# Sliding-window attention into a mixture of attention experts: outputs as rows of tokens with the key sum as a 65th column, fp32 turns, 128-key score products and 768-byte rows of q and k

## The chip, the cores and the metric

The program runs on one core of one Trainium2 chip. The metric is the device time of one execution in microseconds, as the median over runs. A core has TensorE (PE, with its weight loads shown apart as PEld), VectorE (DVE), ScalarE (ACT), GpSimd (POOL) and SyncE (SP), which here issues the DMAs.

## The reference

Eight batches of 576 tokens; the first layer has eight heads of 64, the second four experts with heads of 64.

```python
# layer 1: sliding window, per batch and head
scores = q @ k.T / 8                      # where |i - j| <= 32, else -1e9
attn = softmax(scores);  y = attn @ v
x = y of all heads side by side           # (8, 576, 512)
# layer 2: gate and experts
logits = x @ w_gate                       # 4 experts, the best 2 per token, softmax over the 2
for e in range(4):
    a = softmax(causal((x @ wq[e]) @ (x @ wk[e]).T / 8))
    out += weight_of_e * (a @ (x @ wv[e])) @ wo[e]
```

Everything is float32 outside. The first layer and the gate are computed in fp32, the experts in bf16 with fp32 sums.

## The kernel before

The kernel is written as named steps, and the string `ORDER` lists them in the order in which they are emitted. Every engine works through its own instructions in that order, so `ORDER` also fixes what TensorE does next and which DMA SP issues next. A step such as `S.4.1:21` is "scores of group 4, half 1"; the digits behind the colon choose which of four PSUM slots of two banks each it uses. `wN` is N warm-up products. The function `step` beside each name holds a planner's costs and dependencies; they were used to find the order and don't run on the chip. Groups are i = 2b + g: batch b, four heads each.

The steps of the first layer, with b the batch:

- `load.i.qn` and `load.i.kn` (L138, four DMAs each, on SP): one group's q or k goes to SBUF as `nat`, 32 partitions a head, in rows of two tokens (512 bytes). Groups 0 and 1 come in two parts.
- `turn` (L285): DVE turns 32 x 32 blocks, four instructions a load, so that head dimensions lie on partitions.
- `S.i.half` (L305): per half of 288 queries, products of 64 keys with 64 to 160 queries, each in two pieces of 32 head dimensions; heads take the four row groups of the array, even and odd 64-key blocks its two column halves. Then exp on ACT (L311) and the band mask, a multiply on POOL (L313; on DVE for groups 0 and 1).
- `loadv` (L152, L154, five DMAs) and `dup` (L162 on ACT, L164 on POOL): V in tiles of 128 keys, and copies shifted by 64 so that every span of queries finds its 128 keys on 128 partitions.
- `SUM.b` (L321): the sums over keys, 32 products with one-hot weights, then a reciprocal on DVE. For batches 0 to 3 the reciprocals are split into three bf16 parts (L330 to L335).
- `U.i.x` (L364): output of two heads as 64 dimensions by queries, eight segments of 64 or 96 queries each, V as weights.
- For batches 0 to 3 `U` is copied by ACT (L373), and `N.i.x` spreads the reciprocals over partitions with a selecting product (L384) and multiplies on DVE (L386). For batches 4 to 7 (`SPREAD`) the reciprocals go to DRAM and come back broadcast over 64 partitions (`Ro`, `Ri`; RD and RB), and DVE multiplies straight from PSUM (L368).
- Both leave XTF, the layer's output in fp32 with dimensions on partitions, which the gate reads, and a bf16 copy XTB by POOL (L378) for the experts.

The second layer's steps are `G1` and `G3` (the gate), `QK` and `V` (projections, L450, L472), `PS` (scores and exp, L492, L495), `AV` (L518), `PT` (turns in bf16, L540) and `Y` (output projection, L551, copy by ACT, L556, and the DMA out). `WL` and `WC` load and cast the experts' weights (L245 to L264), once. fp32 products are written as one call and appear in the trace as two matmul records.

Of the kernel before, what the change touches and what calls it, by code (L numbers as in the profile page):

```python
# [8 lines left out]
F32 = mybir.dt.float32  # L9
BF16 = mybir.dt.bfloat16  # L10
# [24 lines left out]
    dup.2.0.3 S.6.0:02 dup.2.0.0 load.7.kn.0 PS.1.0.1:1 AV.0.1:3 SUM.2:2 dup.3.0.3 dup.2.0.2 PS.1.1.0:1
    PS.1.0.2:3 load.8.kn.0 turn.7.kn.0 U.5.1:0 U.4.0:1 PT.0.0:3 dup.3.0.0 load.7.qn.0 S.6.1:02 load.8.qn.0
    U.4.1:1 turn.7.qn.0 N.4.0:0 PS.1.1.1:2 N.5.1:3 U.5.0:1 PS.1.0.3:2 turn.8.kn.0 load.9.kn.0 S.7.0:30
    N.4.1:2 U.6.0:1 PS.1.1.2:0 PT.0.1:3 turn.8.qn.0 N.5.0:2 AV.1.0:1 S.7.1:03 loadv.4.0 G1.2:2 QK.2.0.0:0
    load.10.kn.0 G3.2 S.8.0:31 QK.2.0.1:0 turn.9.kn.0 U.6.1:3 PS.2.0.0:0 load.9.qn.0 turn.9.qn.0 PS.1.1.3:1
    SUM.3:2 S.8.1:10 load.11.kn.0 V.2.0:3 WL.o PS.2.0.1:0 S.9.0:21 PS.2.0.2:0 AV.1.1:3 load.10.qn.0 U.7.0:1  # L40
    V.2.1:0 WC.o QK.2.1.0:2 turn.10.qn.0 PT.1.0:0 turn.10.kn.0 S.9.1:31 QK.2.1.1:2 PS.2.0.3:3 U.7.1:0
    N.6.1:2 PS.2.1.0:3 N.7.0:1 PT.1.1:0 N.7.1:2 load.12.qn.0 N.6.0:3 load.12.kn.0 PS.2.1.1:1 SUM.4:0
    dup.4.0.0 load.11.qn.0 PS.2.1.2:3 QK.3.0.0:1 loadv.5.0 Ro.4 G1.3:2 dup.4.0.2 dup.4.0.3 V.3.0:1
    PS.2.1.3:3 dup.4.0.1 G3.3 QK.3.0.1:0 QK.3.1.0:3 S.10.0:21 turn.11.qn.0 PS.3.0.0:3 load.13.kn.0
    QK.3.1.1:0 V.3.1:2 dup.5.0.2 AV.2.0:1 Ri.4 PS.3.0.1:2 Y.0.0:0 U.8.1:3 PS.3.1.0:1 PS.3.0.2:0 U.8.0:2
    turn.11.kn.0 S.10.1:13 Y.0.2:2 U.9.0:0 S.11.0:31 PS.3.0.3:0 U.9.1:2 PS.3.1.1:3 turn.12.kn.0 load.13.qn.0
# [16 lines left out]
"""  # L63


MASKS = ["DVE"] * 2 + ["POOL"] * 14
DUP = ["ACT", "POOL", "ACT", "POOL"]

SPREAD = (4, 5, 6, 7)

S = 576
HS = 288


@with_exitstack
def kernel(
# [12 lines left out]
    nc = tc.nc  # L89
# [31 lines left out]


    nat = {}
    vsb = {}


    def parts(i):
        return [(0, 5), (5, 9)] if i < 2 else [(0, 9)]
# [577 lines left out]
```

## Time and profile before

| what | before |
|---|---|
| median of 6 runs | 285.15 us (282.73 to 286.09) |
| the profiled execution's own time | 286.83 us |
| its span | 285.1 us |
| PE busy, share of the span | 261.1 us, 92% |
| DVE, ACT, POOL busy | 167.6, 154.3, 145.6 us |
| mean granted TensorE clock | 0.968 |
| moved by DMA | 45.48 MB in 91,800 packets |

The span runs from the first to the last instruction of the program. A busy PE is not a PE at its peak: matmuls are pipelined and their ends are modelled. In the chain of waits "SPq" is time in which the chain hangs on SP's queue of DMA issues, "issue" time in which the engine waited for nothing that the profile shows. Where a stretch is given as A:B, both are microseconds from the start of the span.

### The profile page before, as it was taken

What the parts mean: (1) busy time and instruction counts of PE and PEld (TensorE: products, weight loads), DVE (VectorE), ACT (ScalarE), POOL (GpSimd) and SP (SyncE); (2) the same over time, 40 slices, a digit from 0 to 9 for tenths busy, and PEclk for the clock granted to TensorE, in tenths of its full rate; (3) what the DMA queues carried; (4) which work ended last, traced back from release to release, by engine and by line L of the source; (5) the groups of instructions that cost most, each with busy time, mean ns of one, the idle gap of its engine ahead of it and who ended that gap; (6) DMA issues with size and microseconds to landing.
All of it is one profiled execution on the core that took longest, in us unless ns stands there. A gap on an engine that the chain in (4) does not pass through costs nothing.

```text
span 285.1 us, 12971 instructions
## 1 busy us (share of the span) xinstructions
PE 261.1 (92%) x5723; PEld 188.6 (66%) x5723; DVE 167.6 (59%) x448; ACT 154.3 (54%) x226; POOL 145.6 (51%) x202
## 2 busy tenths in 40 slices
PE   8967959996999799979999999999999999999873
PEld 2533837775787677867776787687768677856520
DVE  5735772364884767757576576448784167454610
ACT  1443333883467773446757643936574753377242
POOL 7103065916759667584644965767545932322200
PEclk9997997998999999999999999999999999999959
DMA  4647999999999758999873596899471204411126
GB/s 127 157 126 190 204 157 214 208 200 202 198 206 191 118 111 180 196 207 147 166 203 126 167 232 115 254 258 226 94 222 41 78 22 143 175 74 57 57 117 215
DMA packets 91800, 45.48 MB, mean 160 GB/s; under 512 B 47840, under 2 KB 84832, under 8 KB 91744
## 3 DMA queue, kind: packets, MB, share of 16 engines
q1 hardware_dynamic: 91744, 44.66, 69.5%
q8 instruction: 44, 0.72, 1.2%
q14 instruction: 12, 0.10, 0.1%
HBM read 35.14 MB, written 9.51 MB: 157 GB/s over the span
## 4 chain that ended last, share of the span: by engine, by line
PE 67%; SPq 17%; DMA 5%; issue 4%; DVE 4%; ACT 2%; ACTq 0%; DVEq 0%
PE u L364 11%; PE sc L305 10%; SPq L138 9%; PE pp L450 9%; PE po L518 8%; PE py L551 7%; PE ps L492 6%; PE pv L472 5%; PE sums L321 4%; DMA kn<-in_k_dram 3%; SPq L152 3%; PE pg L406 3%; PE pt L540 2%; SPq L245 2%; DMA qn<-in_q_dram 2%
## 5 line engine op out<-in xcount | busy, mean ns | idle before, releaser
L313 POOL TENSOR_TENSOR AT<-AT,MASKP 128x576 f32<-128x576 f32 x56 | 77.6, 1408 | 32.9 <-ACT AT L311 32.8
L495 ACT ACTIVATE ATE<-ps 128x1024 bf16<-128x1024 f32 (+1 forms) x64 | 53.0, 837 | 30.9 <-PE ps L492 28.0
L311 ACT ACTIVATE AT<-sc 128x576 f32<-128x576 f32 x64 | 38.1, 648 | 43.6 <-PE sc L305 41.3
L305 PE MATMUL sc<-Tqn,Tkn 32*64 32x128 f32 (+3 forms) x2560 | 48.1, 271 | 9.2 <-DVE Tkn L285 3.9
L305 PEld LDWEIGHTS sc<-Tqn,Tkn 32*64 32x64 f32 x2560 | 41.1, 132 | 17.8 <-issue 7.7
L364 PE MATMUL u<-AT,vsb 128*64 128x64 f32 (+1 forms) x1024 | 40.2, 234 | 5.2 <-issue 5.1
L364 PEld LDWEIGHTS u<-AT,vsb 128*64 128x64 f32 x1024 | 35.1, 140 | 10.1 <-issue 8.2
L378 POOL CAST XTB<-XTF 128x576 bf16<-128x576 f32 x32 | 21.1, 665 | 28.3 <-DVE XTF L368 15.1
L285 DVE STREAM_TRANSPOSE Tkn<-kn 128x288 f32<-128x288 f32 (+2 forms) x72 | 25.5, 412 | 8.4 <-DMA kn<-in_k_dram 8.4
L499 POOL TENSOR_SCALAR_AFFINE_SELECT ATE<-ATE 128x384 bf16<-128x384 bf16 x32 | 15.9, 521 | 26.8 <-ACT ATE L495 26.7
L285 DVE STREAM_TRANSPOSE Tqn<-qn 128x288 f32<-128x288 f32 (+2 forms) x72 | 25.4, 412 | 5.8 <-DMA qn<-in_q_dram 5.7
L556 ACT COPY ysb<-py 128x1024 f32<-128x1024 f32 (+1 forms) x24 | 20.6, 867 | 13.3 <-PE py L551 13.2
L518 PE MATMUL po<-VE,ATE 128*128 128x65 bf16 (+2 forms) x480 | 26.7, 197 | 0.0
L551 PE MATMUL py<-WO,OTT 128*128 128x512 bf16 (+1 forms) x80 | 23.5, 417 | 2.8 <-ACT ysb L556 2.2
L518 PEld LDWEIGHTS <-ATE 128*128 128x128 bf16 (+2 forms) x480 | 21.3, 101 | 6.3 <-issue 2.3
L164 POOL COPY vsb<-vsb 64x512 f32<-64x512 f32 (+2 forms) x18 | 14.3, 796 | 18.3 <-DMA vsb<-in_v_dram 17.6
L492 PE MATMUL ps<-QKE 64*128 64x64 bf16 (+5 forms) x192 | 21.7, 283 | 0.1
L472 PE MATMUL pv<-WV,XTB 128*128 128x256 bf16 (+1 forms) x160 | 20.3, 274 | 0.1
L368 DVE TENSOR_TENSOR XTF<-u,RB 128x576 f32<-128x576 f32 x16 | 12.1, 758 | 12.9 <-PE u L364 10.4
L227 PE MATMUL warm<-WARM 128*128 128x512 bf16 x59 | 18.4, 473 | 1.4 <-POOL WARM L168 1.4
L162 ACT COPY vsb<-vsb 64x1024 f32<-64x1024 f32 (+1 forms) x18 | 17.1, 948 | 3.9 <-DMA vsb<-in_v_dram 3.5
L373 ACT COPY us<-u 128x576 f32<-128x576 f32 x16 | 10.2, 641 | 15.4 <-PE u L364 15.3
(76 smaller groups left out, 323.0 us busy)
## 6 DMA issues: line engine op xcount, KB each, us to landing
out_dram<-ysb SPq DMA_DIRECT2D x16, 512.0 KB, 3.4
kn<-in_k_dram SPq DMA_DIRECT2D x56, 144.0 KB, 4.5
qn<-in_q_dram SPq DMA_DIRECT2D x56, 144.0 KB, 5.3
vsb<-in_v_dram SPq DMA_DIRECT2D x28, 256.0 KB, 5.0
RB<-RD SPq DMA_DIRECT2D x32, 144.0 KB, 3.2
vsb<-in_v_dram SPq DMA_DIRECT2D x15, 128.0 KB, 5.0
out_dram<-ysb SPq DMA_DIRECT2D x8, 128.0 KB, 3.4
qn<-in_q_dram SPq DMA_DIRECT2D x8, 80.0 KB, 2.1
```

Of the source, the lines that this page charges most:

```text
L138: nc.sync.dma_start(t[32 * hh:32 * hh + 32, a0:a1, :, :].rearrange("p a s d -> p a (s d)"), src[b, 4 * g + hh].rearrange("(a p s) d -> p a ...
L285: nc.vector.transpose(T[:, dh, :].rearrange("q (a p s) -> q s a p", p=32, s=2)[:, x, a0:a1], n_[:, a0:a1, x, 32 * dh:32 * dh + 32])
L305: nc.tensor.matmul(sl[hh // 2][64 * par:64 * par + 64, hh % 2, lo - c0:hi - c0], KT[r, dh, k0:k0 + 64], QT[r, dh, lo:hi], start=(dh == 0), ...
L311: nc.scalar.activation(ap, sl[p][:, :, 0:HS], EXP, scale=scale_att)
L313: eng.tensor_tensor(out=ap, in0=ap, in1=MASK[:, None, c0:c0 + HS].to_broadcast([128, 2, HS]), op=MULT)
L364: nc.tensor.matmul(u[64 * x:64 * x + 64, half, lo - HS * half:hi - HS * half], V[:, c, h, :], A[:, h % 4, lo:hi], start=True, stop=True, s ...
L450: nc.tensor.matmul(pp[:, half, 0:HS], WQK[j][n][:, dt, :], XTB[:, dt, HS * half:HS * half + HS], start=(dt == 0), stop=(dt == NDT - 1))
L472: nc.tensor.matmul(o, XTB[:, dt, 128 * t:128 * t + n], WV[:, dt, :], start=(dt == 0), stop=(dt == NDT - 1))
L492: nc.tensor.matmul(ps[0:rows, eo, at:at + hi - lo], QKE[r, 1, 128 * kt:128 * kt + nrow(kt)], QKE[r, 0, lo:hi], start=True, stop=True)
L495: nc.scalar.activation(ATE[0:rows, :, 512 * c:512 * c + w], ps[0:rows, :, 0:w], EXP, scale=scale_moe)
L518: nc.tensor.matmul(po[0:n, eo, 65 * qt:65 * qt + 65], ATE[0:nk, eo, o:o + n], VE[0:nk, kt, 2 * j + eo, :], start=(kt == 0), stop=(kt == qt))
L551: nc.tensor.matmul(py[0:n, t - t0, :], OTT[:, j, 128 * t:128 * t + n], WO[:, j, :], start=(j == 0), stop=(j == 1))
```

## The change

- A load of q or k has rows of three tokens (768 bytes); a turn has six DVE instructions of 192 columns. Only group 0 comes in two parts, and its q is issued by ACT instead of SP.
- V is loaded with an offset of 32 keys into two fixed buffers with a stride of 72, whose 65th column is set to one once, so that tile a holds the 128 keys around queries 64a to 64a + 63. All four `dup` copy two tiles.
- k's turned form lies in fixed buffers with 32 zero columns at each end. Halves of the scores are 256 and 320 queries, and blocks (0), (256) and (512) are products of 128 keys with 128 queries; the others keep 64 keys.
- `U.i.x` now takes the masked scores as weights (64 queries) and V with its column of ones as the moving operand: the result is 64 tokens by 65, the last column being the key sum. DVE takes reciprocals and multiplies into XN, tokens by dimensions. `E.b` does the last 64 tokens of both groups.
- `T.b.dt` turns XN by five fp32 transposes into PSUM; ACT copies to XTF and POOL casts to XTB as before.
- `SUM`, `N`, `Ro`, `Ri` and their constants are gone. The whole order is a new one; the second layer's functions are unchanged.

```diff
 ORDER = """
-    load.0.qn.0 load.0.kn.0 load.1.qn.0 load.1.kn.0 turn.0.qn.0 turn.0.kn.0 load.0.qn.1 loadv.0.0
-    load.0.kn.1 load.1.qn.1 turn.1.qn.0 load.1.kn.1 loadv.0.1 turn.1.kn.0 load.2.kn.0 w18:2 S.0.0:01
-    turn.0.qn.1 dup.0.1.3 w6:2 S.1.0:10 load.2.qn.0 turn.0.kn.1 turn.1.qn.1 turn.1.kn.1 late.0 dup.0.0.0
-    w17:2 S.0.1:01 dup.0.1.2 load.3.kn.0 w3:3 S.1.1:02 dup.0.1.0 turn.2.kn.0 dup.0.1.1 w14:1 SUM.0:2
-    turn.2.qn.0 dup.0.0.3 dup.0.0.1 dup.0.0.2 U.1.0:0 U.0.1:1 turn.3.kn.0 load.3.qn.0 U.0.0:0 N.0.1:1
...
+    load.0.qn.0 load.0.kn.0 loadv.0.0 load.1.kn.0 turn.0.qn.0 load.1.qn.0 turn.0.kn.0 dup.0.0.3 dup.0.0.1
+    dup.0.0.0 dup.0.0.2 load.0.qn.1 w18:2 S.0.0:01 turn.1.kn.0 load.0.kn.1 loadv.0.1 dup.0.1.1 turn.1.qn.0
+    w17:2 U.0.0:1 w8:3 S.1.0:02 turn.0.qn.1 WL.q load.2.qn.0 turn.0.kn.1 dup.0.1.2 dup.0.1.0 load.2.kn.0
+    w9:1 S.1.1:20 load.3.qn.0 dup.0.1.3 S.0.1:13 U.1.0:0 U.1.1:1 E.0:3 WC.q U.0.1:0 T.0.3:3 w1:1 T.0.1:0
+    T.0.0:3 T.0.2:1 turn.2.qn.0 turn.2.kn.0 w8:0 QK.0.0.0:1 load.3.kn.0 WL.v S.2.0:30 turn.3.qn.0
+    turn.3.kn.0 loadv.1.0 load.4.qn.0 QK.0.0.1:1 QK.0.1.0:3 S.3.0:02 PS.0.0.0:3 QK.0.1.1:1 load.4.kn.0 WC.v
+    S.2.1:02 G1.0:1 PS.0.1.0:3 PS.0.0.1:0 V.0.0:2 dup.1.0.3 dup.1.0.1 G3.0 dup.1.0.0 dup.1.0.2 S.3.1:03
+    V.0.1:2 turn.4.qn.0 U.2.0:1 PS.0.1.1:0 turn.4.kn.0 PS.0.0.2:3 U.2.1:2 U.3.0:0 load.5.kn.0 PS.0.1.2:3
+    late.0 U.3.1:1 PS.0.0.3:2 load.5.qn.0 E.1:3 S.4.0:20 T.1.2:3 turn.5.kn.0 T.1.3:1 turn.5.qn.0 T.1.0:2
+    loadv.2.0 T.1.1:0 AV.0.0:3 PS.0.1.3:0 S.4.1:21 G1.1:0 S.5.0:23 G3.1 load.6.qn.0 QK.1.0.0:1 load.8.qn.0
...
-SPREAD = (4, 5, 6, 7)
...
+VW = 72
...
     def parts(i):
-        return [(0, 5), (5, 9)] if i < 2 else [(0, 9)]
+        return [(0, 3), (3, 6)] if i < 1 else [(0, 6)]
...
-            nat[nm, b, g] = natp.tile([128, 9, 2, 64], F32, name=nm, tag=nm)
+            nat[nm, b, g] = natp.tile([128, 6, 3, 64], F32, name=nm, tag=nm)
...
+        i = 2 * b + g
+        a0, a1 = parts(i)[n]
+        eng = nc.scalar if i == 0 and nm == "qn" else nc.sync
         for hh in range(4):
-            nc.sync.dma_start(t[32 * hh:32 * hh + 32, a0:a1, :, :].rearrange("p a s d -> p a (s d)"),
-                              src[b, 4 * g + hh].rearrange("(a p s) d -> p a (s d)", p=32, s=2)[:, a0:a1])
+            eng.dma_start(t[32 * hh:32 * hh + 32, a0:a1, :, :].rearrange("p a s d -> p a (s d)"),
+                          src[b, 4 * g + hh].rearrange("(a p s) d -> p a (s d)", p=32, s=3)[:, a0:a1])
...
+    VS = [consts.tile([128, 9, H, VW], F32, name=f"VS{n}") for n in range(2)]
+
     def load_v(b, n):
+        t = VS[b % 2]
         h = slice(*vparts(b)[n])
+        for m, p0, p1 in ((0, 32, 128), (1, 0, 128), (2, 0, 128), (3, 0, 128), (4, 0, 96)):
+            k0 = 128 * m - 32
+            nc.sync.dma_start(t[p0:p1, 2 * m, h, 0:64],
+                              v[b, h, k0 + p0:k0 + p1, :].rearrange("h p d -> p h d"))
...
+        t = VS[b % 2]
+        h = slice(*vparts(b)[part])
+        lo, m0 = n // 2, 2 * (n % 2)
+        p = slice(0, 64) if lo else slice(64, 128)
+        o = t[p, 2 * m0 + 1:2 * m0 + 4:2, h, 0:64]
+        i = t[p, 2 * (m0 + lo):2 * (m0 + lo) + 3:2, h, 0:64]
...
+    KTS = [consts.tile([128, 2, 640], F32, name=f"KT{n}") for n in range(2)]
+    for n in range(2):
+        nc.vector.memset(KTS[n][:, :, 0:32], 0.0)
+        nc.vector.memset(KTS[n][:, :, 608:640], 0.0)
...
+    MASKP = consts.tile([128, 704], F32, name="MASKP")
+    nc.vector.memset(MASKP, 1.0)
+    for ap in (MASKP[0:64, 0:640], MASKP[64:128, 64:704]):
...
+    nc.vector.memset(MASKP[0:32, 64:128], 0.0)
+    nc.vector.memset(MASKP[96:128, 576:640], 0.0)
+    MASK = MASKP[:, 64:640]
+
+    for n in range(2):
+        nc.vector.memset(VS[n][0:32, 0, :, :], 0.0)
+        nc.vector.memset(VS[n][96:128, 8, :, :], 0.0)
+        nc.vector.memset(VS[n][:, :, :, 64:65], 1.0)
...
     def late_constants():
-        nc.vector.tensor_reduce(NM, nmt, axis=AXX, op=ADD)
         nc.scalar.copy(ident_bf, ident)
-        nc.scalar.copy(SEL[:, :, :, :].rearrange("p j a (h d) -> p (j a h) d", d=64),
-                       sels[:, :, :].rearrange("p j h -> p (j h)")[:, :, None].to_broadcast([128, 32, 64]))
...
-    EBLK = [[(0, 0, 96), (1, 96, 224), (2, 224, 288)], [(2, 288, 352), (3, 352, 480), (4, 480, 576)]]
-    OBLK = [[(0, 0, 160), (1, 160, 288)], [(2, 288, 416), (3, 416, 576)]]
-
-    SEGS = [(0, 96), (96, 160), (160, 224), (224, 288), (288, 352), (352, 416), (416, 480), (480, 576)]
+
+
+    BLK = [[[(0, 128, 0, 128)], [(128, 64, 64, 192), (192, 64, 128, 256)], [(256, 64, 192, 256)]],
+           [[(256, 128, 256, 384)], [(512, 128, 448, 576)], [(384, 64, 320, 448), (448, 64, 384, 512)]]]
+    CUT = [0, 256, 576]
...
-            qt_[b, g, nm] = qkt.tile([128, 2, S], F32, name="T" + nm, tag="T" + nm)
+            qt_[b, g, nm] = (KTS[(2 * b + g) % 2][:, :, 32:608] if nm == "kn" else
+                             qkt.tile([128, 2, S], F32, name="T" + nm, tag="T" + nm))
...
-            for x in range(2):
-                nc.vector.transpose(T[:, dh, :].rearrange("q (a p s) -> q s a p", p=32, s=2)[:, x, a0:a1],
+            for x in range(3):
+                nc.vector.transpose(T[:, dh, :].rearrange("q (a p s) -> q s a p", p=32, s=3)[:, x, a0:a1],
...
-        QT, KT = qt_[b, g, "qn"], qt_[b, g, "kn"]
+        QT, KT = qt_[b, g, "qn"], KTS[(2 * b + g) % 2]
...
+        c0, c1 = CUT[half:half + 2]
+        for blocks in BLK[half]:
             for dh in range(2):
+                for k0, n, lo, hi in blocks:
+                    p0 = k0 % 128
+                        nc.tensor.matmul(sl[hh // 2][p0:p0 + n, hh % 2, lo - c0:hi - c0],
+                                         KT[r, dh, k0:k0 + n], QT[r, dh, lo:hi],
+                                         start=(dh == 0), stop=(dh == 1), skip_group_check=True)
...
+            ap = A[:, 2 * p:2 * p + 2, c0:c1]
+            nc.scalar.activation(ap, sl[p][:, :, 0:c1 - c0], EXP, scale=scale_att)
...
-    def win_sums(b):
-
-        ss = slot("sums")[:, 0, :]
-        for h in range(8):
-            for j in range(4):
-                nc.tensor.matmul(ss[32 * j:32 * j + 32, 0:144], OH[:, h, :],
-                                 AT[b, h // 4][:, h % 4, 144 * j:144 * j + 144],
-                                 start=(h == 0), stop=(h == 7), skip_group_check=True)
-        if b in SPREAD:
...
-            nc.vector.reciprocal(RF, ss[:, 0:144])
...
-    def recip_out(b):
-        RF = st.pop(("RF", b))
...
-    def recip_in(b):
...
-    def win_av(b, pair):
-        A, V = AT[b, pair // 2], vsb[b]
...
+                              in1=MASK[:, None, c0:c1].to_broadcast([128, 2, c1 - c0]), op=MULT)
...
+    XN = consts.tile([128, NQT, DM], F32, name="XN")
+
+    def win_out(o, u, n):
+        rs = smallp.tile([128, n, 4], F32, name="rs", tag=f"rs{n}")
+        nc.vector.reciprocal(rs, u[:, :, :, 64])
+        nc.vector.tensor_tensor(out=o, in0=u[:, :, :, 0:64],
+                                in1=rs[:, :, :, None].to_broadcast([128, n, 4, 64]), op=MULT)
+
+    def win_av(b, g, x):
+        A, V = AT[b, g], VS[b % 2]
+        us = slot("u")
+        for hh in range(4):
+            for t in range(2):
+                for y in range(2):
+                    a = 4 * x + 2 * t + y
+                    nc.tensor.matmul(us[64 * y:64 * y + 64, t, 65 * hh:65 * hh + 65],
+                                     A[:, hh, 64 * a:64 * a + 64], V[:, a, 4 * g + hh, 0:65],
+                                     start=True, stop=True, skip_group_check=True)
+        win_out(XN[:, 2 * x:2 * x + 2, 256 * g:256 * g + 256].rearrange("p t (h d) -> p t h d", d=64),
+                us[:, :, 0:260].rearrange("p t (h c) -> p t h c", c=65), 2)
+
+    def win_av_end(b):
+        V = VS[b % 2]
+        us = slot("u")
+        for hh in range(4):
+            for g in range(2):
+                nc.tensor.matmul(us[64 * g:64 * g + 64, 0, 65 * hh:65 * hh + 65],
+                                 AT[b, g][:, hh, 512:576], V[:, 8, 4 * g + hh, 0:65],
                                  start=True, stop=True, skip_group_check=True)
+        win_out(XN[:, 4:5, 0:256].rearrange("p t (h d) -> p t h d", d=64),
+                us[:, 0:1, 0:260].rearrange("p t (h c) -> p t h c", c=65), 1)
...
+    def win_turn(b, dt):
+        pt = slot("tx")[:, :, :].rearrange("p a c -> p (a c)")
+        for t in range(4):
+            nc.tensor.transpose(pt[:, 128 * t:128 * t + 128], XN[:, t, 128 * dt:128 * dt + 128], ident)
+        r = slice(64 * (dt // 2), 64 * (dt // 2) + 64)
+        nc.tensor.transpose(pt[:, 512:576], XN[r, 4, 128 * (dt % 2):128 * (dt % 2) + 128], ident[r, r])
+        nc.scalar.copy(XTF[:, dt, 0:S], pt[:, 0:S])
...
-    def win_norm(b, pair):
-        RS = st["RS", b]
...
+        nc.gpsimd.tensor_copy(X[b][:, dt, :], XTF[:, dt, 0:S])
...
-                         [("DMA", 2.9 * (a1 - a0) / 9, -1), ("LAT", 1.6, 0)])
+                         [("AQ" if i == 0 and nm == "qn" else "SP", 1.8, -1), ("DMA", 2.3 * (a1 - a0) / 6, 0),
+                          ("LAT", 0.8, 1)])
...
-                step(("S", i, half), lambda b=b, g=g, half=half: win_scores(b, g, half), 1.5,
+                step(("S", i, half), lambda b=b, g=g, half=half: win_scores(b, g, half), 1.25,
...
+                step(("U", i, x), lambda b=b, g=g, x=x: win_av(b, g, x), 1.05,
+                     [(("S", i, h), n) for h in range(x + 1) for n in (1, 3)] +
                      [("dup", b, g if b == 0 else 0, n) for n in range(4)] +
+                     ([("T", b - 1, dt) for dt in range(4)] if b else []),
+                     [("DVE", 0.75, -1)], (0,))
+        step(("E", b), lambda b=b: win_av_end(b), 0.55,
+             [(("S", 2 * b + g, 1), n) for g in range(2) for n in (1, 3)] +
+             [("dup", b, p, n) for p in range(len(vparts(b))) for n in range(4)] +
+             ([("T", b - 1, dt) for dt in range(4)] if b else []), [("DVE", 0.45, -1)], (0,))
+            step(("T", b, dt), lambda b=b, dt=dt: win_turn(b, dt), 0.53,
+                 [("U", 2 * b + dt // 2, x) for x in range(2)] + [("E", b)] + XT,
+                 [("ACT", 0.55, -1), ("POOL", 0.7, 0)], (0,))
...
+                 [("U", 2 * b - 4 + g, x) for g in range(2) for x in range(2)] + [("E", b - 2)] if b > 1 else
+                 [("loadv", b, 0)] if part else [],
+                 [("SP", 2.25, -1), ("DMA", 6.5 * fr, 0), ("LAT", 0.8, 1)])
...
+        X4 = [("T", b, dt) for dt in range(4)]
...
```

## The prediction

> **What bounds the kernel now.** I read the page first: the busy shares, the 40 slices and the chain of waits.
>
> ```profile
> PE 261.1 (92%) x5723; PEld 188.6 (66%) x5723; DVE 167.6 (59%) x448; ACT 154.3 (54%) x226; POOL 145.6 (51%) x202
> PE   8967959996999799979999999999999999999873
> GB/s 127 157 126 190 204 157 214 208 200 202 198 206 191 118 111 180 196 207 147 166 203 126 167 232 115 254 258 226 94 222 41 78 22 143 175 74 57 57 117 215
> PE 67%; SPq 17%; DMA 5%; issue 4%; DVE 4%; ACT 2%; ACTq 0%; DVEq 0%
> ```
>
> TensorE looks full, but the chain gives it two thirds; the rest is mostly SP's queue. The second view, busy time by stretches, separates the stages.
>
> ```profile
> 0.00:57.30 57.30, 47.92 (x995) 31.14 (x995) 30.68 (x84) 24.30 (x43) 24.73 (x43) 0.94 0.82 173
> 57.30:270.00 212.70, 204.96 (x4708) 154.79 (x4707) 134.81 (x357) 124.87 (x178) 120.90 (x160) 0.99 0.70 156
> 270.00:285.10 15.10, 8.19 (x26) 2.68 (x25) 2.13 (x7) 5.10 (x6) 0.00 (x0) 0.73 0.43 157
> ```
>
> The columns are the stretch, its length, then PE, PEld, DVE, ACT and POOL busy with counts, clock, DMA share and GB/s. The middle stretch is TensorE's: 204.96 of 212.7 us, and no other engine is above 135. The last one is the tail of output projections. In the first, TensorE's 48 us contain 18.4 us of warm-up products (L227), so it waits for data. The third view, the chain in order of time, says for which data.
>
> ```profile
> 48.97 0.82 SPq L154
> ...
> 52.54 4.17 DMA kn<-in_k_dram
> 56.70 1.04 ACT vsb L162
> 57.79 1.09 PE u L364 x28
> ```
>
> L154 is the last issue of `loadv.1`; after it come the copies of V and the products of batch 1, and from there TensorE runs almost without a hole. The data of `loadv.1` end at about 52 us in the packet records. So there are three terms: when batch 1's V is there, TensorE's work after that, and its idle time.
>
> **What the Trainium skill says.** "TensorE: Matmul & The Clock Gate", section Terms, says that the transpose mode makes fp32 four times faster. The trace has no fp32 transpose; its fp32 products leave two matmul records each (L364: 1024 records for 512 products). The same page, section LDWEIGHTS, has the load go by columns, not rows. That agrees: 32 fp32 columns take 110 ns (L321), 64 take 132 to 140 (L305, L364). "TensorEngine Tiling (Array Packing)", Key Properties, says that changing the tiling mode drains the array. That agrees too: in the bf16 turns of L540 the first four starts are 56 ns apart, and the fifth, with 64 rows, starts 147 ns after the fourth. "DMA: Bandwidth & Descriptors", Specifications, wants 512 bytes or more for line rate. Here V's 256-byte rows moved as fast as q's and k's 512-byte rows, about 200 GB/s, so I take the trace.
>
> **The start (0 to 57.3 us).** Before `loadv.1` has landed, these have to move: four groups of q and k, 8 x 0.59 = 4.72 MB; V of two batches, 2.36 MB; weights 1.58 MB; 8.66 MB in all. Now that takes until 52 us, for two reasons. SP needs 0.47 us an issue, and parts of 5 and 4 blocks keep it below the engines' rate: 132 and 152 GB/s in the first two stretches of 12 us, 198 in the third. Second, the weights come before V with rows of 256 bytes.
>
> ```profile
> 0.80 1.84 SPq L138 DMA_DIRECT2D qn<-in_q_dram  x4
> 2.68 1.87 SPq L138 DMA_DIRECT2D kn<-in_k_dram  x4
> ...
> 33.78 5.14 SPq L251 DMA_DIRECT2D tmpv<-in_moe_wv_dram  x4
> ...
> 44.42 4.51 SPq L152 DMA_DIRECT2D vsb<-in_v_dram  x4
> ```
>
> After the change SP issues 60 DMAs up to there instead of 76: group 1 is no longer in parts (-8), and group 0's q (8) goes to ACT's queue beside SP's. From some 3 us on the engines and no longer the issue set the rate. At 198 GB/s throughout, 8.66 MB take 43.7 us, and from 1.8 us on that is 45.5. The larger rows may give more: a 512-byte packet took 42 ns and a 2,048-byte one 95, and a line through both puts 768 bytes at 51 ns, 243 GB/s over 16 engines. Then q and k take 19.4 us instead of 23.8 and V lands at 41. If a packet's time goes by bytes alone, nothing is gained. I take 43, that is 9 earlier than 52, with bounds of 41 and 47.
>
> Is TensorE ready by then? Group 3 lands some 8.5 us before V (1.7 MB at 200 GB/s), at 34.5; two turns of 1.6 us bring its scores to 38. From there to `U.2.0` come 1.3 x 3 for scores, 1.06 for a projection, 1.23 for the gate, 2.4 for V's projection and 3 x 0.32: 9.6 us, so 47.6. V at 43 plus the same 5.3 us from landing to products as now (52 to 57.3) gives 48.3. Both say 48.4, 8.9 us earlier. Behind either there is not much: if V came at 38, the scores' path would still hold the start at 47.
>
> **TensorE's work from there to the last `AV`.** Durations are from start to start of the next step in the trace. Removed: 7 `SUM` x 2.10 = 14.7; 12 `N` x 0.35 = 4.2 (batches 1 to 3; the others have their sums by way of DRAM and none). Two `PS` and one `PT` fall outside: 1.1. `U` keeps 16 products in 8 pairs, 32 records. Pairs of 64 columns follow each other in 58 ns and pairs of 96 in 82; with 65 columns everywhere 16 x 59 and the change of tile of 0.15 make 1.09 instead of 1.16: 28 x 0.07 = 2.0. Added: 7 `E` with half the pairs, 8 x 59 + 0.12 = 0.59 each, 4.1. `S` has 64 products instead of 80. At two cycles a column and two records a product, its levels stream 1.07 and 1.28 us for the two cuts, against 1.17 and 1.28 for the blocks of now; but a 128-key product takes all four column groups, and each half changes its tile once inside. I leave it at 1.32; 1.25 and 1.42 are the ends, 24 x that is -1.7 to +2.4.
>
> `T` is the unknown, 28 of them. The nearest row is the bf16 turn `PT` with the same five pieces, 0.45. Below, an fp32 transpose in one pass that streams like bf16 pays only one longer load behind the change of tile: 0.53, which is also what the diff's own planner puts. If each 128-column load shows, 58 ns doubled, 4 x 0.112 and the fifth piece make 0.77. If it takes two records as the products do, ten levels of 0.112 and 0.1 make 1.22. I take 0.60: 16.8 us. Sum: -14.7 - 4.2 - 1.1 - 2.0 + 4.1 + 16.8 = -1.1 us. The key sums leave, and turning the outputs costs nearly all of it.
>
> **Idle time in that stretch** is 10.4 us: the steps' own times sum to 202.35 against 212.75 from `U.3.0` to the end of `AV.7.1`. Its largest pieces stand ahead of `U`, such as this one in the chain:
>
> ```profile
> 64.82 1.01 PE u L364 x27
> 65.82 2.23 issue
> 68.06 0.39 PE u L364 x5
> ```
>
> The products have waited for a masked tile from POOL there (its L313 took 65.57 to 68.33). The new `U` of x=0 needs only the first half of its scores, which eases that. New waits stand against it: `T` waits for `E`, whose multiply is queued on DVE behind the turns, and the next batch's `U` can't write XN before all four `T` have read it; behind such a multiply on DVE stand turns and projection copies, for which PE waits in turn. The order puts a score step or more between. I take 8.4, that is 2 less, from 4 to 14.
>
> **The other engines** have room. DVE loses 37 us (sums 13.9, normalizing 11.4 and 12.1) and gains 32 x (0.21 + 0.69) for `U`, 8 x 0.6 for `E` and 6 for turns in six pieces instead of four: +2. ACT gains 32 x 0.64 and loses 16 x 0.64 and 1.9 of SEL: +8. POOL gains 8 x 0.4 in the copies of V. All stay under 175 us. RD and RB, 4 x 8 broadcasts of 144 KB, leave DMA engines that are below their limit then (61 to 180 GB/s in most stretches after 160 us). The tail behind `AV.7.1` has the same steps and is bound by ACT's copies of 1.01 us: no change.
>
> **Sum.** 8.9 + 1.1 + 2.0 = 12 us less. The profiled execution's own time was 286.83 (span 285.1, 1.7 around it), and gives 274.8. It was 0.6% above the median of 285.15; on that the forecast is 273.2.
>
> **Rivals.** (1) The transposes take two records. At 1.22 instead of 0.60 the 28 of them add 17.4 and those of batch 0 about 1 at the start: 273.2 + 18.4 = 291.6, slower. For it speaks that every fp32 product here leaves two records; against it the skill's sentence. It decides from `T` = 0.60 + 12/28 = 1.03 us on. (2) The start gains little: rows of 768 bytes cost by bytes, the two queues share the same engines, V lands at 47, `U.2.0` starts at 52.4, and the idle time stays at 10.4: 285.15 - 4.9 - 1.1 = 279.2. The early windows below 160 GB/s speak against it. (3) Both unknowns fall well: `T` 0.53 and `S` 1.25 save 2 + 1.7, and idle falls to 5.5, 2.9 more: 266.6. For it: shorter dependencies of `U`. Against it: `E` and `T` add eight steps a batch that wait for DVE or ACT.
>
> **How the numbers follow.** Forecast 0.55, rival 1 0.12, rival 2 0.19, rival 3 0.14. The range has to reach rivals 2 and 3 with their spread (V at 41 to 47, idle 4 to 14, `S` at 1.42), and leaves out rival 1: 263 to 284. A measurement of this kernel can tell about 1%, 2.85 us: below 282.3 lie the forecast and rival 3, and nearly all of rival 2: 0.85; within 1%: 0.05; slower, from rival 1 and its mixtures with a good start: 0.10.
>
> **What would show it.** Right: the first `U` of batch 1 near 48 us, the third 12-us stretch no longer the first one near 200 GB/s; one matmul record for a transpose and 0.5 to 0.8 us from a `T` to the next step; `U` at 1.09, `S` near 1.32; DVE, ACT and POOL all under 175 us. Wrong: two records for a transpose, or 0.11 us between its pieces twice over; scores over 1.42; idle time in the middle stretch over 14 us, with `T` or `U` behind it waiting for DVE.

## The result, and the profile after

| | before | after |
|---|---|---|
| median | 284.85 us (62 runs) | 280.71 us (27 runs, 278.55 to 284.19) |
| ratio, with its 95% interval | | 0.9893 (0.987 to 0.9917) |
| span of the profiled execution | 285.1 us | 280.6 us |

The change makes the kernel 1.1% faster. 273.2 was forecast; the range holds the result, but only a third of the gain came. The medians below are over all executions; the ratios leave out those over 1.5% above the fastest of their kernel, in most of which TensorE's clock was lower, and of the run `s64` only one of six is left then, so it is read by its steps.

First the page of the changed kernel: busy TensorE, its 40 slices, the rate of the DMAs and the chain of waits.

```profile
PE 267.5 (95%) x4925; PEld 192.3 (69%) x4925; DVE 170.8 (61%) x538; ACT 162.6 (58%) x241; POOL 145.6 (52%) x190
PE   8989999999999999999999999999999999999762
GB/s 149 234 205 210 197 193 219 213 203 222 219 186 201 202 217 135 215 117 50 127 134 200 166 101 175 168 167 2 77 97 77 2 21 2 78 149 43 72 119 217
PE 78%; SPq 6%; DMA 6%; DVE 5%; ACT 2%; issue 1%; ACTq 0%; DVEq 0%
```

TensorE has 798 records less than before and is nevertheless busy 6.4 us longer. The slices are nines from the fourth one to the tail, and "issue" in the chain fell from 4% to 1%. The stretches (length, busy times, clock, DMA share, GB/s, as before), cut at the first `U` of batch 1 and behind the last `AV`:

```profile
0.00:50.10 50.10, 46.52 (x830) 30.69 (x831) 32.46 (x106) 24.64 (x44) 19.38 (x29) 1.00 0.93 202
50.10:264.60 214.50, 212.12 (x4069) 158.16 (x4067) 135.74 (x424) 132.81 (x192) 126.20 (x162) 0.99 0.60 131
264.60:280.60 16.00, 8.84 (x31) 3.48 (x30) 2.59 (x8) 5.11 (x6) 0.00 (x0) 0.71 0.41 147
```

The start shrank by 7.2 us, the middle grew by 1.8, and in it TensorE is busy 212.1 of 214.5 us. Adding up the middle step by step (number of steps times the median from a step's start to the next one's) separates work from idle time:

| term, us | forecast | measured |
|---|---|---|
| start, to the first `U` of batch 1 | -8.9 | -7.2 (57.3 to 50.1) |
| TensorE's steps from there | -1.1 | +11.1 (203.0 to 214.1) |
| time in that stretch beyond the medians | -2.0 | -9.3 (9.7 to 0.4) |
| behind it | 0 | +0.9 |
| sum | -12.0 | -4.5 |

`U` takes 1.08 us (1.09 forecast) and `E` 0.57 (0.59). Two step kinds are larger than forecast: `S` takes 1.52 us for half 0 and 1.73 for half 1, both 1.32 before, so 12 x (0.20 + 0.41) = 7.3 us; `T` takes 0.79 instead of 0.60, 28 x 0.19 = 5.3. And nearly all time beyond the medians is gone. The costliest groups on the page, after and then before (line, tile, shape, count, busy us, mean ns, idle ahead of it and its releaser):

```profile
L289 PE MATMUL sc<-Tqn,KT 32*64 32x128 f32 (+2 forms) x2048 | 55.2, 276 | 1.3 <-DVE Tqn L273 0.9
L289 PEld LDWEIGHTS sc<-Tqn,KT 32*64 32x64 f32 (+1 forms) x2048 | 44.8, 151 | 11.6 <-issue 3.4
L316 PE MATMUL u<-VS,AT 128*64 128x65 f32 x1024 | 36.6, 225 | 0.7 <-PE u L327 0.4
```

```profile
L305 PE MATMUL sc<-Tqn,Tkn 32*64 32x128 f32 (+3 forms) x2560 | 48.1, 271 | 9.2 <-DVE Tkn L285 3.9
L364 PE MATMUL u<-AT,vsb 128*64 128x64 f32 (+1 forms) x1024 | 40.2, 234 | 5.2 <-issue 5.1
```

The score products became fewer and their busy time grew by 7.1 us. The idle time of 5.1 us in front of `U` was put down to "issue" before, to no engine and no load. So there were three questions: what lengthens `S`, what lengthens `T`, and which idle time went.

### The profile page after: what moved, and what is told of

The parts are those of the page before. It is cut to its first block, busy times and chain, and to the rows that moved or that the text cites. A ratio compares the mean times of both kernels' runs of the same rounds, so it can differ in the third digit from the quotient of the medians.

```text
span 280.6 us, 11400 instructions
## 1 busy us (share of the span) xinstructions
PE 267.5 (95%) x4925; PEld 192.3 (69%) x4925; DVE 170.8 (61%) x538; ACT 162.6 (58%) x241; POOL 145.6 (52%) x190
## 4 chain that ended last, share of the span: by engine, by line
PE 78%; SPq 6%; DMA 6%; DVE 5%; ACT 2%; issue 1%; ACTq 0%; DVEq 0%
PE sc L289 16%; PE pp L405 10%; PE po L473 9%; PE u L316 9%; PE py L506 7%; PE tx L337 6%; PE pv L427 6%; PE ps L447 5%; DMA qn<-in_q_dram 4%; SPq L136 3%; PE pg L361 3%; PE pt L495 3%; PE tx L339 2%; SPq L152 2%; PE u L327 1%
## 5 line engine op out<-in xcount | busy, mean ns | idle before, releaser
L296 POOL TENSOR_TENSOR AT<-AT,MASKP 128x512 f32<-128x512 f32 (+1 forms) x56 | 77.6, 1408 | 41.4 <-ACT AT L294 41.1
L294 ACT ACTIVATE AT<-sc 128x512 f32<-128x512 f32 (+1 forms) x64 | 38.2, 648 | 37.1 <-PE sc L289 37.1
L289 PE MATMUL sc<-Tqn,KT 32*64 32x128 f32 (+2 forms) x2048 | 55.2, 276 | 1.3 <-DVE Tqn L273 0.9
L289 PEld LDWEIGHTS sc<-Tqn,KT 32*64 32x64 f32 (+1 forms) x2048 | 44.8, 151 | 11.6 <-issue 3.4
L316 PE MATMUL u<-VS,AT 128*64 128x65 f32 x1024 | 36.6, 225 | 0.7 <-PE u L327 0.4
L316 PEld LDWEIGHTS u<-VS,AT 128*64 128x64 f32 x1024 | 32.9, 138 | 5.7 <-issue 3.8
L273 DVE STREAM_TRANSPOSE KT<-kn 128x192 f32<-128x192 f32 (+1 forms) x102 | 29.2, 392 | 3.0 <-DMA kn<-in_k_dram 1.8
L273 DVE STREAM_TRANSPOSE Tqn<-qn 128x192 f32<-128x192 f32 (+1 forms) x102 | 29.2, 393 | 2.9 <-DMA qn<-in_q_dram 2.4
L343 POOL CAST XTB<-XTF 128x576 bf16<-128x576 f32 x32 | 20.8, 667 | 17.2 <-ACT wsink L214 11.1
L306 DVE TENSOR_TENSOR XN<-u,rs 128x512 f32<-128x512 f32 (+1 forms) x40 | 25.5, 638 | 1.4
L337 PE MATMUL tx<-ident,XN 128*128 128x128 f32 x128 | 20.9, 285 | 0.3 <-DVE rs L305 0.3
```

The costliest lines, as they stand in the source:

```text
L273: nc.vector.transpose(T[:, dh, :].rearrange("q (a p s) -> q s a p", p=32, s=3)[:, x, a0:a1], n_[:, a0:a1, x, 32 * dh:32 * dh + 32])
L289: nc.tensor.matmul(sl[hh // 2][p0:p0 + n, hh % 2, lo - c0:hi - c0], KT[r, dh, k0:k0 + n], QT[r, dh, lo:hi], start=(dh == 0), stop=(dh == 1 ...
L294: nc.scalar.activation(ap, sl[p][:, :, 0:c1 - c0], EXP, scale=scale_att)
L296: eng.tensor_tensor(out=ap, in0=ap, in1=MASK[:, None, c0:c1].to_broadcast([128, 2, c1 - c0]), op=MULT)
L306: nc.vector.tensor_tensor(out=o, in0=u[:, :, :, 0:64], in1=rs[:, :, :, None].to_broadcast([128, n, 4, 64]), op=MULT)
L316: nc.tensor.matmul(us[64 * y:64 * y + 64, t, 65 * hh:65 * hh + 65], A[:, hh, 64 * a:64 * a + 64], V[:, a, 4 * g + hh, 0:65], start=True, s ...
```

## Experiments

### Scores back to 64 keys, and full-tile turns

`s64` has only blocks of 64 keys:

```diff
-    BLK = [[[(0, 128, 0, 128)], [(128, 64, 64, 192), (192, 64, 128, 256)], [(256, 64, 192, 256)]],
-           [[(256, 128, 256, 384)], [(512, 128, 448, 576)], [(384, 64, 320, 448), (448, 64, 384, 512)]]]
+    BLK = [[[(0, 64, 0, 64), (64, 64, 0, 128)], [(128, 64, 64, 192), (192, 64, 128, 256)], [(256, 64, 192, 256)]],
+           [[(256, 64, 256, 320), (320, 64, 256, 384)], [(384, 64, 320, 448), (448, 64, 384, 512)],
+            [(512, 64, 448, 576), (576, 64, 512, 576)]]]
```

> Undone: the 128-key score products; all score blocks have 64 keys again, in pairs for the two halves of the partitions, with the cut at 256 kept. Theory 1 (the mis-sized score step: the changed kernel's TensorE has no idle time from 50 us on, and its scores cost 1.52 and 1.73 us a half where they cost 1.32 and 1.32): the two halves fall back to about 2.64 us together, 0.61 less, 12 times in the middle stretch = 7.3 us, and up to 9.8 if the four groups of the start count: 271 to 273.4 us. Theory 2 (the idle time of the kernel before came from TensorE's instruction fetch, and went because there are fewer instructions): the records of TensorE rise from 4925 to about 5690, as many as before, and holes inside steps come back, 5 to 8 us in the middle stretch: 276 to 280 us.

`t128` takes the fifth piece of `T` with 128 rows; `ident2` is the identity with its column halves swapped:

```diff
-        nc.tensor.transpose(pt[:, 512:576], XN[r, 4, 128 * (dt % 2):128 * (dt % 2) + 128], ident[r, r])
+        nc.tensor.transpose(pt[:, 512:640], XN[:, 4, 128 * (dt % 2):128 * (dt % 2) + 128], (ident, ident2)[dt // 2])
```

> The fifth piece of the fp32 transposes of the outputs (64 rows of 64) is taken as all 128 rows in one 128x128 transpose, for dt 2 and 3 with an identity whose halves are swapped, so that the wanted 64 columns come first; the copy to XTF is unchanged. No step changes the tile any more. Theory 1 (the two tile changes cost 0.2 us of the step's 0.79): a T takes 0.57 to 0.62, 28 x 0.19 = 5.3 us less in the middle stretch, 275.5 us. Rival (the transposes' own streaming and the wait for XN or the PSUM slot set the step's length): 0.76 to 0.80 as now, within 1 us of 280.7.

> Both edits, 64-key score blocks and full-tile transposes. If TensorE's work is all that bounds the stretch, the gains add: 7.3 (to 9.8) + 5.3, 265.6 to 268 us. If a further bound lies close behind (ACT at 133 of 214 us, DVE at 136, the q and k loads), the sum falls short by 3 us or more.

| run | median, us | ratio to before | `S` halves, us | `T`, us | beyond the medians, us |
|---|---|---|---|---|---|
| after | 280.71 | 0.9893 | 1.52, 1.73 | 0.79 | 0.4 |
| `t128` | 275.48 | 0.9697 (0.9637 to 0.9757) | 1.52, 1.73 | 0.60 | 0.3 |
| `s64` | 277.38; the other five 285.51 to 291.25 | | 1.22, 1.44 | 0.79 | 10.0 (in one of 288.26) |
| `s64t128` | 276.27 | 0.9689 (0.9626 to 0.9753) | 1.22, 1.44 | 0.60 | 7.7 |

**The turns.** `t128` does what its first theory said: `T` falls to 0.60 and the median by 5.2 us. In the order in time, after and then `t128` (start, length, instruction):

```profile
148.36 0.66 PE L337 MATMUL tx<-ident,XN 128*128 128x128 f32 x4
148.94 0.27 PE L339 MATMUL tx<-ident,XN 64*128 64x64 f32 x1
149.15 0.66 PE L337 MATMUL tx<-ident,XN 128*128 128x128 f32 x4
```

```profile
146.36 0.60 PE L340 MATMUL tx<-ident,XN 128*128 128x128 f32 x4
146.80 0.27 PE L341 MATMUL tx<-ident,XN 128*128 128x128 f32 x1
146.91 0.60 PE L340 MATMUL tx<-ident,XN 128*128 128x128 f32 x4
```

With one tile the fifth piece starts 0.44 us behind the first and the next step 0.11 behind it. With the 64-row tile the fifth piece begins 0.58 behind the first, and the next step's first piece 0.21 behind the fifth. From record to record a piece is 109 ns and the two around the small tile are 203 each: a change of tile costs 94 ns, twice a step, and the first piece behind it takes 165 ns instead of 109. In `t128` a `T` right behind another takes 0.55 us. The small piece has half the rows of a full one and, with the change, takes nearly twice as long.

**The scores.** The medians of `s64` are the expected ones: 2.66 us for both halves. One half 0 of the same group, after and in `s64t128`:

```profile
135.53 1.59 PE L289 MATMUL sc<-Tqn,KT 32*128 32x128 f32 x64
```

```profile
138.10 1.29 PE L293 MATMUL sc<-Tqn,KT 32*64 32x64 f32 x80
```

64 records take longer than 80. A level is a set of products that run side by side, the four heads in their row groups. From record to record, both forms run through eight levels of some 110 ns on average and four of half that, for the block with 64 queries: a product of 128 keys (tile 32*128) has all the array's columns to itself, where a pair of 64-key blocks (tile 32*64) shares them. So the larger products stream nothing faster. What they add is three gaps: the first level takes 213 ns instead of 112, the first 64-key level starts 220 ns behind the last 128-key one, and that level takes 160 instead of 110. That is 0.26 of the 0.30 us a half. The Trainium skill, "TensorEngine Tiling (Array Packing)", Key Properties, says that a change of the tiling mode drains the array; these runs agree, and put it at 94 to 108 ns a change, with 50 to 56 more on what comes first behind it.

**But the gain of `s64` is not there.** In `s64t128` the steps' medians sum to 7.0 us less than in `t128`, and the time beyond them is 7.3 us more: no gain in the median. Theory 2 of `s64` holds, and the sum expected of `s64t128` falls short by 8 us or more. The groups on the page of `s64t128` have the idle time back, in front of scores and named "issue"; the second fence is its order in time, with a hole inside a step, behind its 56th of 80 records:

```profile
L293 PE MATMUL sc<-Tqn,KT 32*64 32x128 f32 (+1 forms) x2816 | 47.9, 259 | 9.5 <-issue 5.3
```

```profile
68.02 1.03 PE L293 MATMUL sc<-Tqn,KT 32*64 32x64 f32 x56
70.56 0.49 PE L293 MATMUL sc<-Tqn,KT 32*64 32x128 f32 x24 [1.50 <-issue]
```

No product of a score step waits for anything that the first 56 did not wait for. What does come at these times is an instruction fetch, a packet of 16 KB on a queue of its own. The number of fetches goes with TensorE's records. The page's DMA queues (packets, MB, share of the engines' time), before and then after:

```profile
q8 instruction: 44, 0.72, 1.2%
```

```profile
q8 instruction: 38, 0.62, 1.0%
```

5723 records in 44 fetches and 4925 in 38 are 130 records each; `s64` and `s64t128` have 5693 weight loads, one for each of TensorE's records, and 44 fetches. Two things tie the holes to the fetches. In the packet records every hole of over 0.3 us that is named "issue" and lies inside a step between 57 and 255 us, 14 in the kernels before and after and in these two, ends 1.2 to 1.9 us behind the last byte of such a fetch; the one shown ends 1.3 behind it. And the holes stand at fixed places of the program: a hole that ends behind fetch n has 127.9 n + 91 of TensorE's records ahead of it in the kernel before (all four), and 127.4 n + 90 in `s64` and `s64t128` (all nine), each to within one record. The distance, 127.4 or 127.9 records a fetch, is nearly what a fetch brings, so I read these places as the borders between two blocks of instructions. Ahead of 13 of the 14 the last 130 records had taken only 2.0 to 4.2 us (5.4 ahead of the smallest, 0.31 us, in the changed kernel). Between 57 and 255 us a fifth of the records comes that fast in the kernels with holes, and 2% in the changed one.

### Is it the dependency of `U`?

`uboth` gives back to `U` its need of both score halves:

```diff
-                    a = 4 * x + 2 * t + y
+                    a = 2 * ((x, 3 - x)[t] if b else 2 * x + t) + y
-        win_out(XN[:, 2 * x:2 * x + 2, 256 * g:256 * g + 256].rearrange("p t (h d) -> p t h d", d=64),
+        win_out(XN[:, (slice(0, 4, 3), slice(1, 3))[x] if b else slice(2 * x, 2 * x + 2), 256 * g:256 * g + 256].rearrange("p t (h d) -> p t h d", d=64),
```

> Same work; in batches 1 to 7 the two U steps of a group share their row tiles otherwise: x=0 takes tiles 0 and 3, x=1 tiles 1 and 2, so that each needs both halves of the scores and their masks, as U did in the kernel before. Theory A (the idle time went because U of x=0 needs only the first half): idle time comes back, up to the 8.9 us that went, 284 to 289 us. Theories B (instruction fetch) and C (order of the steps): within 1.5 us of 280.7.

284.10 us, ratio 0.9992 (0.9957 to 1.0027) to the kernel before. The median lies at the lower end of theory A's range; by the ratios it is 1% slower than the changed kernel, 2.8 us, between the theories. (The 8.9 us of the expectation are the 9.3 of the table above.) The order in time shows what it is, one step:

```profile
220.91 0.34 PE L316 MATMUL u<-VS,AT 128*64 128x65 f32 x4
222.34 0.69 PE L316 MATMUL u<-VS,AT 128*64 128x65 f32 x16 [1.09 <-POOL AT L296]
223.83 0.57 PE L316 MATMUL u<-VS,AT 128*64 128x65 f32 x12 [0.81 <-POOL AT L296]
```

`U.15.0` waits for POOL's masks and takes 3.43 us instead of 1.08, here in an execution of 286.3 us. This wait bears the name of its releaser. So the shorter dependency is worth some 2.4 us at this one place of the new order, and that is a part of the gain; it is not what took away the holes named "issue".

### Is the fetch late because of the data?

`before_noload` is the kernel before, `s64noload` is `s64`, both without most loads of q and k:

```diff
     def load(b, g, nm, n):
+        if 2 * b + g > 2:
+            j = 2 * b + g - 3
+            nat[nm, b, g] = nat[nm, j // 2, j % 2]
+            return
```

> The kernel before without the loads of q and k of groups 3 to 15 (their turns read the tiles of groups 0 to 2 again; all other work as it was, the results are not the reference's): 7.7 MB less through the DMA engines. It asks what makes the 9.7 us of holes inside TensorE's steps, each of which ends 1.2 to 1.8 us behind the landing of a 16 KB fetch of instructions. If the fetches are late because they stand behind the data, their 1.0 to 1.4 us fall and most of the holes between 57 and 260 us go: 2 us or less is left. If a fetch takes its 2.5 to 3 us whatever else moves, the holes stay, 5 to 10 us in all. If they were waits for loads or turns of q and k after all, they go entirely, and so do those at score steps.

> s64 (all score blocks of 64 keys, 5693 records of TensorE) without the loads of q and k of groups 3 to 15 (their turns read the tiles of groups 0 to 2 again; the results are not the reference's). In s64 the score steps hold 7.8 us of time beyond their medians. If the instruction fetches are late because of the data in front of them, as before_noload says (6.2 us of holes inside the steps of the middle stretch there became 1.3), 1 to 3 us are left; if that fall was chance, 6 us or more.

The page's groups of `before_noload` (L368 is `U`), and then of `s64noload` (L294 is `S`):

```profile
L368 PE MATMUL u<-AT,vsb 128*64 128x64 f32 (+1 forms) x1024 | 38.2, 230 | 0.8 <-DVE XTF L390 0.7
```

```profile
L294 PE MATMUL sc<-Tqn,KT 32*64 32x128 f32 (+1 forms) x2816 | 46.8, 259 | 4.3 <-issue 2.4
```

`before_noload`: the 5.1 us of "issue" in front of `U` are gone. In its middle stretch the time beyond the medians falls from 9.7 to 3.2 us, and of the holes inside steps, 5.7 us in four, one of 1.28 us is left, behind 130 records in 2.0 us. It took 275.7 us, 9 less than the kernel before. `s64noload`: its score steps hold 1.4 us beyond their medians and all its steps 1.0; 274.47 us. In `s64` these were 7.8 and 10.0, but at a lower clock; in `s64t128`, whose profile shows the clock at 1.00 from 50 to 250 us as that of `s64noload` does, the score steps hold 6.0. (The loads left out are 15.3 MB and not the 7.7 of the expectation: 30.12 MB moved instead of 45.48.) Each is one execution, but both say the same: with the same instructions and without that data most of the holes go.

The fetch loses the time ahead of its packet. With the borders placed as above, I took the time from TensorE's passing one border to the start of the packet that must be there at the next; from 57 to 130 us its mean is 1.9 us in the kernel before and 0.7 without the loads, 1.8 in `s64t128` and 0.9 in `s64noload`. The packet itself takes 1.37 us before and 1.13 without the loads. An estimate from these: 1.9 + 1.4 + 1.2 to 1.9 makes 4.5 to 5.2 us that a block must last, and 3.0 to 3.7 without that data. The 130 records ahead of nearly all holes took less, 2.0 to 4.2 us.

### The start

`rows512` has q and k in 512-byte rows again (`s=2`, tiles of `[128, 9, 2, 64]`, four turns), and `qsp` issues group 0's q on SP:

```diff
-        return [(0, 3), (3, 6)] if i < 1 else [(0, 6)]
+        return [(0, 5), (5, 9)] if i < 1 else [(0, 9)]
```

```diff
-        eng = nc.scalar if i == 0 and nm == "qn" else nc.sync
+        eng = nc.sync
```

> The changed kernel with q and k in rows of 512 bytes again (two rows of tokens for each packet, turned in four pieces; group 0 in parts of 5 and 4 blocks of 64 tokens), everything else as it is, group 0's q on ACT's queue included. Theory 1 (the larger rows gained what the packets' durations say: 57.4 ns for 768 bytes against 42.0 for 512, that is 2.15 us less for the first 4.72 MB): the first U of batch 1 is 2 us later or less, 280.7 + 1 to 2 us; DVE's turns are 16 x 2 x 0.15 cheaper and hidden. Rival (the larger rows made the whole 7.2 us of the earlier start): 286 to 288. Second rival (TensorE's own work from 36 us on holds the start now): no change, within 1 us.

> The changed kernel with group 0's q issued by SP again instead of ACT. 8 more issues of 0.47 us on SP ahead of V: 3.8 us later for what SP issues behind them, unless the DMA engines and no longer the issues set the rate. If SP's issues set it: first scores 1.9 us later, first U of batch 1 2 to 3.8 us later, 283 to 284.5. If the engines' rate or TensorE's own work holds the start: within 1 us of 280.7.

`rows512`: 280.73 us, 0.9905 (0.9872 to 0.9938), the same as the changed kernel. The last of V's bytes came at 46.1 us instead of 45.2 (52.8 before), the first `U` of batch 1 at 50.6 instead of 50.1. That is no difference: in `uboth` and `tail3`, with the changed kernel's loads, V's last bytes came at 46.4 and the first `U` at 50.4 and 52.0. The second rival's "no change" holds. A 768-byte packet took 57.4 ns from 12 to 44 us, that is 214 GB/s over 16 engines, and a 512-byte one here 44.5, 184 GB/s; nothing of it is seen at V or at `U`. The skill's page "DMA: Bandwidth & Descriptors", Specifications, sets line rate at 512 bytes and more; the 256-byte packets of V and the weights took 19.4 ns in the same time, 211 GB/s, so no run here shows that threshold.

`qsp`: 282.49 us, 0.9933 (0.9903 to 0.9962), 0.4% over the changed kernel, less than the 1% that can be told apart. V's last bytes came at 48.3, in an execution of 287.24 us, and a score step waited (the waits of TensorE from 36 to 56 us: total, times, longest):

```profile
PE sc L289 <- DVE KT L273: 2.5, 1, 2.5
```

With all early loads on one queue V came 2 to 3 us later than in the changed kernel and the runs with its loads (45.2 to 46.4). The first `U` of batch 1 came at 55.5, with the clock at 0.78 and 0.88 from 36 to 56 us; in the time that is 1 to 2 us, if anything. So ACT's queue explains 2 to 3 of V's 7.6 us; the new order of the loads and group 1 in one part weren't tried by themselves.

### Keeping both gains, and the tail

64-key scores only for groups 8 to 15, whose steps run where less data moves, on top of `t128`; then with 128-key products in two of their steps; then with another PSUM slot for the last `AV`:

```diff
-        for blocks in BLK[half]:
+        for blocks in (BLK if 2 * b + g < 8 else BLK64)[half]:                                            # hyb8
+        for blocks in (BLK if 2 * b + g < 8 or (2 * b + g, half) in ((9, 0), (12, 1)) else BLK64)[half]:  # hyb8b
...
-    Y.5.4:1 AV.7.1:0
+    Y.5.4:1 AV.7.1:3                                                                                      # tail3
```

> Full-tile transposes as in t128, and 64-key score blocks for groups 8 to 15 alone (their score steps run from about 104 us on); groups 0 to 7 keep the 128-key products. If 64-key scores cost 0.30 less a half and the holes inside steps come only where TensorE reads instructions faster than they are fetched (late in s64t128 they were 1.0 and 0.7 us, early 1 to 1.9 us each), 16 x 0.30 = 4.8 us less than t128's 275.5 and 0.7 to 1.7 given back: 271.4 to 272.5 us. If the holes move along with the 64-key blocks, as many for a step as in the early groups (0.33 us a score step), nothing is gained: 275 to 276.

> hyb8 with 128-key products also in the two score steps in which all kernels with 64-key blocks had a hole (S.9.0: 1.2 to 1.3 us, S.12.1: 1.0 us). If a hole belongs to a place at which a block of instructions is read too fast, both go and do not turn up elsewhere: 1.2 + 1.0 - 0.6 = 1.6 us less than hyb8's 273.8, 272.2. If they move to other 64-key steps, since the borders of the 16 KB blocks move with the number of instructions: no gain, 273.4 to 274.4.

> The changed kernel with the last AV step's PSUM slot 3 instead of 0, one word of the order. Its AV.7.1 waits 1.51 us at 260.7 us for DVE, because AV.7.0, two short steps ahead, uses the same slot and DVE's three operations on it have to read it first. Theory (that wait lies on the path to the end): 1.2 to 1.5 us less, 279.2 to 279.5. Rival (the tail's chain of AV.7.1, PT, Y and copies on ACT is bound by DVE's OE steps, queued one behind the other, whatever slot AV has): within 0.5 us of 280.7.

> hyb8b and tail3 together. If both hold: 272.2 - 1.4 = 270.8. If the holes move and the wait for the slot lies on the path: 272.4. If neither holds: 273.8.

| run | median, us | ratio to before |
|---|---|---|
| `hyb8` | 273.80 | 0.9656 (0.9603 to 0.9708) |
| `hyb8b` | 273.06 | 0.9653 (0.9588 to 0.9719) |
| `tail3` (on the changed kernel) | 278.22 | 0.9812 (0.9767 to 0.9856) |
| `best` | 270.98 | 0.9563 (0.9519 to 0.9608) |

`hyb8` gains 1.7 us over `t128`, between its two expectations and less than the 1% that can be told apart; its steps say why: `S.9.0` takes 2.63 us instead of 1.22 and `S.12.1` 2.46 instead of 1.44, which gives back 2.4 of the 4.8 us. In `s64` and `s64t128` the same two steps take 2.1 to 2.5. `hyb8b` heals both and has 0.3 and 1.5 us more in `S.15.1` and `S.14.1` instead: the holes move to other dense steps, as its second expectation said. Its median, 0.7 us lower, lies below that one's range and above the first one's, and can't be told from that of `hyb8`.

`tail3` gained more than its 1.2 to 1.5 us, 2.5. The last `AV`, after and in `tail3`:

```profile
262.19 2.47 PE L473 MATMUL po<-VE,ATE 128*128 128x65 bf16 x30 [1.51 <-DVE OE L482]
```

```profile
262.42 1.67 PE L473 MATMUL po<-VE,ATE 128*128 128x65 bf16 x30
```

Of its 2.5 us the wait is 1.5; the rest is not settled. The profiled clock behind 260 us was 0.5 to 0.7 in the changed kernel and 1.00 to 270 us here, which fits the longer products of the upper line: in `t128`, with the same wait and the clock at 1.00, the last `AV` takes 1.59 us to the next step. `best` puts the parts together: 270.98 us, 4.4% faster than the kernel before and 3.3% faster than the changed one (0.9563 / 0.9893).

## Why the prediction was right and wrong

- **The bound.** Right: TensorE set the middle, and no other engine got over 171 us.
- **Start: mis-sized by 1.7 us.** V's last bytes were forecast for 43 us and came at 45.2, inside the bounds of 41 to 47; runs with the same loads show up to 46.4. That is the case without a gain from larger rows, 45.5. The failing number is the line through two packet sizes: 51 ns for 768 bytes, measured 57.4; 6144 packets of q and k by 6.4 ns over 16 engines are 2.5 us. From V to `U` it went about as forecast (5.3 forecast, from 52 us; with the last byte at 52.8 it was 4.5 before, and 4.9 now): the last copy of V on ACT ended at 50.07 us, and TensorE came to `U.2.0` at 50.09. Removing the rows alone (`rows512`) costs nothing in the time, so they were not what made the start.
- **`S` left at 1.32: wrong by 7.3 us.** "Each half changes its tile once inside" stood there, with the price of such a change from the trace beside it (147 ns instead of 56 in the bf16 turns), and was then not multiplied: the ends 1.25 and 1.42 both lie under the 1.52 and 1.73 measured. And "a 128-key product takes all four column groups" was seen but not followed: as many levels as before, whatever the number of products.
- **`T` at 0.60: wrong by 5.3 us.** One record for a transpose, right; the first rival (two records, 1.22) is out. The middle value, 0.77, was nearly right: a piece takes 109 ns, 112 there; that the weight load sets this isn't shown. The 0.60 taken instead is what `T` takes with no change of tile at all (`t128`).
- **Idle time, -2 forecast, -9.3 measured: right sign, wrong cause.** The hole at 65.82 was shown as "issue" and explained by POOL's masks, because POOL was busy at the same time. The prediction's own numbers speak against it: those masks ended at 68.33, and the products went on at 68.06. They belong to `S.4.0`, which ran just before; the step with the hole is `U.2.0`, of another group. The hole stands between the 27th and the 28th record of the step, at a border of two blocks of instructions. By the runs above it was TensorE waiting for instructions, which no view names. Four such holes make 5.7 of the 9.7 us (10.4 in the prediction's count); another 1.7 or so, by my estimate, is a lowered clock (0.84 and 0.78 between 66 and 75 us in the profile before), the rest small ones. The 128-key scores, with fewer records, keep them away: in `t128` against `s64t128` that is worth 7.3 us and costs 7.0. The new `U`, which needs only half the scores, is worth some 2.4 (`uboth`).
- **Tail, no change forecast: +0.9.** The steps behind the last `AV` are the same, at a lowered clock in both profiles; the 0.9 wasn't traced. What the prediction missed lies just ahead: the last two `AV` share a slot in the new order, and the second waits 1.5 us.

The errors cancelled in part, by luck: +7.3 and +5.3 in the work, with 0.4 less in its other steps, against -7.3 in idle time. The signs named as "would show it wrong" were the right ones for `S` ("over 1.42"); for `T`, 0.5 to 0.8 was allowed, too wide to warn.

## What to carry to other kernels

Price every change of tile inside a step, also inside the one that is "only rearranged": about 0.1 us here, so that a small piece with a tile of its own can cost more than a full one. Fewer and larger products gain nothing in streaming if they fill the same columns, but they spare instructions: where a stretch runs 130 of TensorE's records in some 4 us or less while data fills the DMA engines, look for idle time named "issue" in the middle of a step, for a 16 KB fetch in front of it, and for the same distance in records from hole to hole. Explain a hole by what ends it, not by what is busy beside it.

## What the runs showed that was not expected

- Dense small products outrun the instruction fetch: 16 KB for about 130 records, holes of 0.3 to 2.2 us inside steps, each at a border of two such blocks and 1.2 to 1.9 us behind a fetch's last byte; 6.0 us in the score steps of `s64t128`, 1.4 in those of `s64noload`, without most of the q and k loads.
- A turn of 64 x 64 in its own tile takes 203 ns, with 94 more for the change back; one of 128 x 128 in fp32 takes 109.
- The best kernel mixes both kinds of scores: 64-key blocks in the groups that run where less data moves, 128-key products where much does.
